# Convolving parts two at a time in a fused convolution and mixture-of-experts kernel, with 36 instead of 44 pair blocks

## The chip, the core and the metric

The kernel runs on one core of a Trainium2 chip. Five engines work at once and meet through semaphores: TensorE (PE in the profile, with its weight loads as PEld), VectorE (DVE), ScalarE (ACT), GpSimd (POOL) and SyncE (SP), which issues most transfers. The metric is the device time of one execution in microseconds; less is better.

## What is computed

The input has 8 sequences of 3584 tokens with 192 channels. A causal convolution with 7 taps comes first. Its weights are a softmax over the taps and are shared by the 24 channels of a head. Every token then goes to one of 8 experts:

```python
w = softmax(weight, axis=-1)                       # (8 heads, 7 taps)
y[b,s,h*24+c] = sum_k w[h,k] * xpad[b,s+k,h*24+c]
logits = y @ w_gate                                # 8 experts
local  = sigmoid(y @ w_local)
e[b,s] = argmax(logits) if s == 0 or local < 0.5 else e[b,s-1]
out    = softmax(logits)[e] * (relu(y @ w1[e]) @ w2[e])   # 192 -> 1024 -> 192
```

Everything is in 32-bit floats. The choice of expert runs along the sequence, so the tokens have to be routed in order.

## The kernel before

**Parts.** The 28672 tokens are cut into 16 parts of 1792 (128 partitions of 14 tokens). Parts 0 and 1 are convolved on TensorE at the start (`wide`). Parts 2 to 15 are convolved by `conv`: for each of 8 heads ScalarE makes the first tap (L411) and VectorE adds the other six in a chain of `scalar_tensor_tensor` (L421), each over 14 tokens x 24 channels = 336 elements per partition. `route` then computes the logits of a part (`logits`: four VectorE transposes, 48 TensorE products at L618, ScalarE's `ls` copies at L623, VectorE's `lq` transpose at L626, 16 small `lt` copies at L638 or L640), chooses experts, gives each token a slot, and puts 14 groups of rows into `to_put`. `put` (L824) sends one of these from the part's result tile to the DRAM tensor `slots` with an indirect transfer issued by GpSimd.

**Blocks.** As soon as enough tokens of an expert lie in `slots`, they make a block. First come 28 blocks of one unit (128 rows), then `PAIRED` = 44 blocks of two units ("pairs": `hidden`, `output`), then 22 blocks of four units (512 rows: `seven`, `output_late`), and at the end 5 pairs and single units (`hidden_late`, `output_late`). A block loads its expert's weights (`wb`, 1.5 MB) and its rows (`xg`, or `y_sb` in `ring` for the late blocks), transposes the rows, multiplies by w1, applies relu, multiplies by w2, scales, and `deliver` (L1070) scatters the result to the output. `seven` replaces the 8 products of 2x2 pieces of the first layer by 7, with sums that GpSimd (`combine_w`) and VectorE (`combine_x`, L1213, L1216, L1226) form.

**Order.** The order of the work is written out by hand. Within each block, `step(time)` puts pieces of `route` or `conv` into VectorE's queue: 4.8 after the hidden layer of a pair, 1.2 after its output matmuls and 3.6 behind its `o_sb` sums (L1057), and 2.4, 5.4, 2.0 and 1.8 in a block of four (`SIDE`). A piece says what it counts for: a tap of `conv` 0.6. The late blocks carry an overrun over to the next step; the pairs do not. `"hop"` ends a turn of `route` and lets `conv` have the rest of the step, `"pe"` does so until the next step that may use TensorE. `start_conv` lets a part begin when no row that still has to be put belongs to the part whose tile it takes. `ensure` issues the loads of rows up to `AHEAD` = 3 blocks ahead.

**Rooms.** The results of parts lie in four tiles `ys[0..3]`, taken in turn (`row_tile`); from part 8 on three of them turn, and the fourth is the ring of rows for the late blocks. The input `x_sb` has two buffers; `conv` issues the load of part g+1 at its fifth head.

Of the kernel before, what the change touches and what calls it, by code (L numbers as in the profile page):

```python
# [8 lines left out]
F32 = mybir.dt.float32  # L9
# [8 lines left out]
P = 128  # L18
B, S, D = 8, 3584, 192
H, KC = 8, 7  # L20
E, F = 8, 1024
GS = D // H
N = B * S
UT = 128
NT = 14
PT = P * NT
# [38 lines left out]
PADS = NPART  # L65
NARROW = 8
PAIRED = 44
LEFT4 = E * (QT // 2 + UT // 8)
# [42 lines left out]
def kernel(  # L111
    ctx: ExitStack,
    tc: tile.TileContext,
    x: bass.AP,
    xb: bass.AP,
    weight: bass.AP,
    wh: bass.AP,
# [7 lines left out]
    xs = ctx.enter_context(tc.tile_pool(name="xs", bufs=2))  # L125
    ys = [ctx.enter_context(tc.tile_pool(name=f"ys{k}", bufs=1)) for k in range(4)]
    yt = ctx.enter_context(tc.tile_pool(name="yt", bufs=1))
# [17 lines left out]
    def load_x(g):  # L145
        x_sb = xs.tile([P, NX, D], F32, name="x_sb")
        src = x[g // PER]
        win = bass.AP(tensor=src.tensor, offset=src.offset + g % PER * PT * D,
                      ap=[[NT * D, P], [1, NX * D]])
        nc.sync.dma_start(out=x_sb.rearrange("p t d -> p (t d)"), in_=win)  # L150
        return x_sb
# [68 lines left out]

    def z_tile():
        return yt.tile([P, 3 * NH * TB + NB * DR], F32, name="z")

    WIDE = 23

    def wide(g, xv, y_sb, both):
# [55 lines left out]
        yield from convolve(0, range(H))  # L282
        zy = z_tile()
        yT = zy[:, :3 * NH * TB].rearrange("p (u s) -> p u s", s=TB)
# [110 lines left out]

    def row_tile(g):
        at = g % 4 if g < NARROW else (g + 1) % 3
        return ys[at].tile([P, NB, DG], F32, name="y_sb")

    def conv(g, x_sb):  # L400
        y_sb = row_tile(g)[:, :NT, :]
        got[g] = y_sb

        def cols(h):
            return y_sb[:, :, Y0 + h * GS:Y0 + (h + 1) * GS]

        def chans(h, k):
            return x_sb[:, k:k + NT, h * GS:(h + 1) * GS]

        def first(h):  # L410
            nc.scalar.activation(cols(h), chans(h, 0), Act.Copy, scale=c[:, h, 0:1])  # L411

        first(0)
        yield 0
        for h in range(H):
            if h + 1 < H:
                first(h + 1)
            if h == H // 2 and 2 < g < NPART - 1:
                x_in[g + 1] = load_x(g + 1)
            for k in range(1, KC):  # L420
                nc.vector.scalar_tensor_tensor(cols(h), chans(h, k), c[:, h, k:k + 1],  # L421
                                               cols(h), Alu.mult, Alu.add)
                yield 0.6

# [174 lines left out]
    def logits(g, y_sb):  # L599

        z = z_tile()[:, :NT * D].rearrange("p (t d) -> p t d", d=D)
        for t in range(0, NT, TQ):
# [25 lines left out]
        lt = sm.tile([P, NT + 2, E + 1], F32, name="lt")  # L628
        aside = g > EARLY + 2
        for r in range(4):  # L630
            for j in range(4):
# [7 lines left out]
                else:  # L639
                    nc.vector.tensor_copy(dst, src)  # L640
                    yield 0.12
            if aside:
                yield "hop"
# [298 lines left out]
    blocks += [(1, 2, i, next(g for g in range(NPART) if i < TWO[g])) for i in range(TWO[-1])]  # L942
    FIRST = len(blocks)
    blocks += [(2, 4, i, next(g for g in range(NPART) if i < MID[g])) for i in range(MID[-1])]
    blocks += [(3, 4, i, LAST) for i in range(FOUR)]
# [136 lines left out]
    def ring(i):  # L1082

        if "rows" not in room:
            room["rows"] = ys[3].tile([P, NB, DG], F32, name="y_sb").rearrange("p b d -> p (b d)")
        at = (i - FIRST) % 4 * KQ * DG
        return room["rows"][:, at:at + KQ * DG].rearrange("p (k d) -> p k d", d=DG)

# [142 lines left out]
    def output_late(n, wb, xg, hT, rows_next=None, between=None):  # L1231

        for part, h in enumerate(hT):
# [38 lines left out]
    st = {"block": 0, "conv": 1, "cgen": None, "route": 1, "rgen": None, "routed": 1,  # L1272
          "due": False, "since": 0, "bank": None, "over": 0}

    def start_conv():
        g = st["conv"] + 1

        free = not any(p[0] <= g - 3 for p in to_put)
        if (st["cgen"] is None and g < NPART and g <= st["route"] + LEAD and free
                and (g != 3 or g in x_in and st["block"] > LATE + 2)):  # L1280
            st["conv"] = g
            st["cgen"] = conv(g, x_in.pop(g))
            next(st["cgen"])

    def conv_op():
        c = next(st["cgen"], None) if st["cgen"] else None
        if c is None:
            st["cgen"] = None
        return c

    def start_route():
        done = st["conv"] - (st["cgen"] is not None)
        if st["rgen"] is None and st["route"] < done:
            st["route"] += 1
            st["rgen"] = route(st["route"])
# [34 lines left out]

    ya, yb = row_tile(0), row_tile(1)
    hot = hotp.tile([P, 2, NB, UT], F32, name="hot")
# [33 lines left out]
    def ensure(i):  # L1366

        for j in range(len(xgs) + i, min(i + AHEAD + 1, len(blocks))):
            g = blocks[j][3]
# [45 lines left out]
    for i, (_, n, _, _) in enumerate(blocks):  # L1415
# [15 lines left out]
        if i < FIRST:  # L1431
            hT = hidden(n, wbs[i], xT, (1, 1) if i else (0, 0))
            if i < FIRST - 1:
                xT, copied = turn(n_next, xgs[i + 1])
                if len(to_put) > NT // 2 and n == KT:
                    put(copied)
# [95 lines left out]


def _block_layout(np, x):

# [43 lines left out]
```

## Time and profile before

| quantity | value |
|---|---|
| median of 4 runs | 1300.29 us (1299.66 to 1304.92) |
| the profiled execution | 1301.73 us, of which 1299.9 us is the span from the first to the last instruction |
| granted TensorE clock, mean | 0.996 |
| 0 to 211 us: parts 0 to 2, single units | PE busy 201.5 of 211.0 us |
| 211.3 to 695 us: the 44 pairs | PE busy 483.7 of 483.7 us, DVE 412.6, ACT 261.1, POOL 206.2 |
| 695 to 927 us: blocks of four beside convolution and routing | PE busy 229.8 of 232.0 us, DVE 193.9, ACT 139.8 |
| 927 to 1152.9 us: the other blocks of four | PE busy 225.9 of 225.9 us, DVE 111.4, ACT 126.0 |
| 1152.9 to 1300 us: last pairs and single units | PE busy 135.4 of 147.1 us |

The page gives each engine's busy time and the costliest groups of instructions. The view by stretches gives the same for chosen stretches of the span, and the view of waits who waited for whom. A TensorE instruction's end is modelled, so what counts is when the next one starts. A busy engine that no one waits for costs nothing.

### The profile page before, as it was taken

Reading aid. Unit: us, or ns where it says so; the run is one execution under the profiler, and the core shown is the slowest. Engines: PE = TensorE matmul, PEld = TensorE weight load, DVE = VectorE, ACT = ScalarE, POOL = GpSimd, SP = SyncE. Lnnn points to the kernel's source line nnn. Section 1 sums busy time; section 2 is a strip of 40 time slices with the busy share of each in tenths; the row PEclk is TensorE's granted clock in tenths of the full one; section 3 lists DMA queues with packets and bytes.
Section 4 is the critical chain, followed back from the end, with each engine's and each line's share of the span. In section 5 each row is a group of like instructions: output and inputs, shape, how many; then the busy total and the mean of one; then the engine's idle time right before and its main releaser. Section 6 shows DMA issues by size and latency. Waiting matters only on the chain.

```text
span 1299.9 us, 40433 instructions
## 1 busy us (share of the span) xinstructions
PE 1276.6 (98%) x16218; PEld 1233.5 (95%) x16218; DVE 908.9 (70%) x2513; ACT 703.9 (54%) x1573; POOL 547.4 (42%) x615
## 2 busy tenths in 40 slices
PE   9899999999999999999999999999999999999996
PEld 7799999999999999999999999999999999999996
DVE  6989898888888888798888888988378433310000
ACT  5456564545564646556465666575655556544453
POOL 4455352434434344444436625534536643321111
PEclk9999999999999999999999999999999999999998
DMA  5899998757766657767674435243433433325684
GB/s 198 292 348 417 389 380 323 271 195 257 271 245 221 254 209 269 268 210 266 211 282 153 167 137 172 97 143 115 150 123 129 160 105 135 111 99 187 238 305 160
DMA packets 59619, 281.52 MB, mean 217 GB/s; under 512 B 11680, under 2 KB 31191, under 8 KB 43554
## 3 DMA queue, kind: packets, MB, share of 16 engines
q1 hardware_dynamic: 37104, 233.66, 50.0%
q0 software_dynamic: 22320, 45.22, 9.4%
q8 instruction: 130, 2.13, 0.7%
q14 instruction: 63, 0.52, 0.1%
q10 hardware_dynamic: 2, 0.00, 0.0%
HBM read 233.25 MB, written 46.07 MB: 215 GB/s over the span
## 4 chain that ended last, share of the span: by engine, by line
PE 86%; issue 7%; DVE 3%; POOL 1%; DMA 1%; POOLq 0%; ACT 0%; SPq 0%; DVEq 0%
PE yps L1043 24%; PE hps L1024 23%; PE ps L1243 18%; PE ps L1194 13%; PE xps L1194 3%; PE xps L392 2%; POOL out_dram L1070 1%; PE hps L618 1%; DVE y_sb L421 1%; PE ps L1144 1%; DMA wb<-in_w_dram 1%; DMA out_dram<-o_sb,y_sb 1%; PE hps L242 1%; PE hps L187 0%; DVE hot L584 0%
## 5 line engine op out<-in xcount | busy, mean ns | idle before, releaser
L421 DVE SCALAR_TENSOR_TENSOR y_sb<-x_sb,c,y_sb 128x336 f32<-128x336 f32 x672 | 382.7, 578 | 39.0 <-ACT y_sb L411 21.3
L1043 PE MATMUL yps<-wb,hT 64*128 64x192 f32 x3712 | 323.4, 326 | 2.1 <-DVE o_sb L1057 2.0
L1024 PE MATMUL hps<-xT,wb 64*128 64x256 f32 (+1 forms) x3456 | 319.3, 336 | 1.7 <-DVE at L513 1.2
L1043 PEld LDWEIGHTS yps<-wb,hT 64*128 64x128 f32 x3712 | 305.0, 188 | 3.8 <-DVE o_sb L1057 2.3
L1024 PEld LDWEIGHTS hps<-xT,wb 64*128 64x128 f32 x3456 | 285.4, 187 | 24.2 <-issue 3.0
L1243 PE MATMUL ps<-wb,hot 64*128 64x192 f32 x3616 | 303.9, 323 | 0.0
L824 POOL DMA_INDIRECT slots<-y_sb,posi x228 | 226.3, 993 | 169.9 <-ACT xT L1010 72.3
L1243 PEld LDWEIGHTS ps<-wb,hot 64*128 64x128 f32 x3616 | 296.4, 187 | 0.7 <-issue 0.6
L1070 POOL DMA_INDIRECT out_dram<-o_sb,y_sb x113 | 117.2, 1037 | 294.6 <-DVE o_sb L1258 279.4
L1070 POOL DMA_INDIRECT out_dram<-o_sb,xg x116 | 120.8, 1041 | 240.7 <-DVE o_sb L1057 196.7
L1031 ACT ACTIVATE hT<-hps 128x512 f32<-128x512 f32 (+1 forms) x288 | 132.3, 511 | 153.2 <-PE hps L1024 153.2
L1258 DVE SCALAR_TENSOR_TENSOR o_sb<-ps,y_sb,o_sb 128x192 f32<-128x192 f32 x113 | 42.4, 411 | 206.6 <-ACT o_sb L1253 199.5
L1253 ACT ACTIVATE o_sb<-ps,y_sb 128x192 f32<-128x192 f32 x113 | 42.2, 418 | 148.9 <-PE ps L1243 144.8
L1053 ACT ACTIVATE o_sb<-yps,xg 128x192 f32<-128x192 f32 x116 | 44.0, 418 | 131.4 <-PE yps L1043 131.4
L1010 ACT COPY xT<-xps 64x256 f32<-64x256 f32 (+4 forms) x288 | 106.8, 371 | 9.6 <-PE xps L392 5.2
L1124 ACT COPY xT<-xps 64x512 f32<-64x512 f32 (+6 forms) x168 | 86.2, 513 | 2.2
L1194 PE MATMUL ps<-xT,wb 64*128 64x256 f32 x704 | 84.8, 376 | 0.0
L1194 PEld LDWEIGHTS ps<-xT,wb 64*128 64x128 f32 x704 | 73.7, 187 | 1.6 <-issue 0.3
L1144 PE MATMUL ps<-xT,wb 64*128 64x128 f32 (+1 forms) x960 | 70.1, 298 | 1.2 <-DMA wb<-in_w_dram 1.2
L1144 PEld LDWEIGHTS ps<-xT,wb 64*128 64x128 f32 x960 | 68.1, 188 | 1.8 <-ACT o_sb L1253 1.3
L1057 DVE SCALAR_TENSOR_TENSOR o_sb<-yps,xg,o_sb 128x192 f32<-128x192 f32 x116 | 44.1, 411 | 31.1 <-ACT o_sb L1053 30.7
L411 ACT ACTIVATE y_sb<-x_sb,c 128x336 f32<-128x336 f32 x112 | 63.0, 580 | 0.5
(283 smaller groups left out, 1335.7 us busy)
## 6 DMA issues: line engine op xcount, KB each, us to landing
wb<-in_w_dram SPq DMA_DIRECT2D x110, 1536.0 KB
x_sb<-in_x_dram SPq DMA_DIRECT2D x14, 1920.0 KB
xg<-slots SPq DMA_DIRECT2D x44, 195.0 KB
y_sb<-slots SPq DMA_DIRECT2D x22, 390.0 KB
wb<-in_w_dram SPq DMA_DIRECT2D x12, 512.0 KB
slots<-y_sb,posi POOLq DMA_INDIRECT x228
x_sb<-in_xb_dram SPq DMA_DIRECT2D x4, 768.0 KB
xg<-slots SPq DMA_DIRECT2D x26, 97.5 KB
```

Of the source, the lines that this page charges most:

```text
L411: nc.scalar.activation(cols(h), chans(h, 0), Act.Copy, scale=c[:, h, 0:1])
L421: nc.vector.scalar_tensor_tensor(cols(h), chans(h, k), c[:, h, k:k + 1], cols(h), Alu.mult, Alu.add)
L824: ins = nc.gpsimd.indirect_dma_start(out=slots[:, :], in_=rows, in_offset=None, out_offset=bass.IndirectOffsetOnAxis(ap=to, axis=0)).ins
L1010: copied = nc.scalar.copy(a, b)
L1024: ins = nc.tensor.matmul(hps[half][:, j, w], lhsT=wb[rows, f0:f0 + P], rhs=xT[rows, d, w], start=(d == 0 and j == 0), stop=(d == KD - 1), ...
L1031: relu = nc.scalar.activation(hT[:, m:m + 2, w], hps[half][:, :, w], Act.Relu)
L1043: ins = nc.tensor.matmul(yps[half][:, k * D:(k + 1) * D], lhsT=hT[rows, m, k * P:(k + 1) * P], rhs=wb[rows, WA + m * D:WA + (m + 1) * D], ...
L1070: sent = nc.gpsimd.indirect_dma_start(out=out, in_=o, in_offset=None, out_offset=bass.IndirectOffsetOnAxis(ap=xg.bitcast(I32)[:, k, IX:], ...
L1124: copied = nc.scalar.copy(a, b)
L1144: nc.tensor.matmul(hps[:, half, j, :], lhsT=wb[rows, f0:f0 + P], rhs=xT[rows, d, :], start=(d == 0 and j == 0), stop=(d == KD - 1), skip_g ...
L1194: ins = nc.tensor.matmul(to[:, half, j, :], lhsT=b[rows, j * P:(j + 1) * P], rhs=a[rows, :], start=(first and j == 0), stop=True, skip_gro ...
L1243: ins = nc.tensor.matmul(yps[:, half, k * D:(k + 1) * D], lhsT=h[two][rows, side, j, k * P:(k + 1) * P], rhs=wb[rows, WA + f * D:WA + (f + ...
```

## The change

- Parts 6 to 15 are convolved two at a time. One unit `(g, g+1)` goes through the 8 heads; each instruction now covers both parts, 28 x 24 = 672 elements. The planner counts 1.0 for such a tap. Parts 2 to 5 are convolved as before. Each part is still routed by itself, but only once its unit is done (`st["done"]`).
- The input of these parts comes from a new array `xd`, laid out by head on the host, so that one `x_sb` buffer holds heads 0 to 3 of both parts and the next heads 4 to 7. Loads are issued at the third and the seventh head.
- The four result tiles become one tile `rooms` for 4 x 14 rows and one tile `third` for 14 rows. A unit takes half of `rooms`; `ROOM` says where, `CLEAR` which parts have to be routed and put before. `z` gets a smaller tile, and the big `z` of the start lies in `rooms`.
- The ring of late rows lies in `third`: three places of four units instead of four; blocks of four look 2 blocks ahead instead of 3.
- The 16 `lt` copies of a part go to ScalarE only while a convolution is under way, else to VectorE, and they are cut by two hops into groups of eight, not by four into groups of four.
- A put behind a pair's row copies is made when more than 2 groups wait, before when more than 7.
- 36 pairs instead of 44, and so 26 blocks of four instead of 22.

```diff
-NARROW = 8
-PAIRED = 44
+WIDER = 6
+PAIRED = 36
@@ load_x
+        if g >= WIDER:
+            nc.sync.dma_start(out=x_sb.rearrange("p t d -> p (t d)"), in_=xd[g - WIDER])
+            return x_sb
...
+    rooms = ys.tile([P, 4 * NT, DG], F32, name="y_sb")
+    third = ys.tile([P, NT, DG], F32, name="y3")
...
-    def row_tile(g):
-        at = g % 4 if g < NARROW else (g + 1) % 3
-        return ys[at].tile([P, NB, DG], F32, name="y_sb")
-
-    def conv(g, x_sb):
-        y_sb = row_tile(g)[:, :NT, :]
-        got[g] = y_sb
+    UNITS = [(g,) for g in range(2, WIDER)] + [(g, g + 1) for g in range(WIDER, NPART, 2)]
+    ROOM = {2: None, 3: 3 * NT, 4: 0, 5: NT}
+    CLEAR = {2: -1, 3: 0, 4: 0, 5: 1}
+    for u, parts in enumerate(UNITS):
+        if len(parts) > 1:
+            ROOM[parts[0]] = (1 - u % 2) * 2 * NT
+            CLEAR[parts[0]] = parts[0] - 3
+    next_x = list(range(4, NPART))
+
+    def conv(parts):
+        g, n = parts[0], len(parts)
+        y2 = (third if ROOM[g] is None else rooms[:, ROOM[g]:ROOM[g] + n * NT, :]).rearrange(
+            "p (a t) d -> p a t d", a=n)
+        for a in range(n):
+            got[g + a] = y2[:, a]
...
         def chans(h, k):
-            return x_sb[:, k:k + NT, h * GS:(h + 1) * GS]
+            if n == 1:
+                return x_in[g][:, k:k + NT, h * GS:(h + 1) * GS]
+            x_sb = x_in[g + h // HH].rearrange("p t d -> p (t d)").rearrange(
+                "p (h a t c) -> p h a t c", h=HH, a=n, c=GS)
+            return x_sb[:, h % HH, :, k:k + NT, :]
...
-            if h == H // 2 and 2 < g < NPART - 1:
-                x_in[g + 1] = load_x(g + 1)
+            if h in ((H // 2,) if n == 1 else (HH // 2, HH + HH // 2)) and g > 2 and next_x:
+                x = next_x.pop(0)
+                x_in[x] = load_x(x)
...
-                yield 0.6
+                yield 0.6 if n == 1 else 1.0
@@ logits
-        aside = g > EARLY + 2
+        aside = g > EARLY + 2 and st["cgen"] is not None
...
-            if aside:
+            if aside and r % 2:
                 yield "hop"
@@ ring
-        at = (i - FIRST) % 4 * KQ * DG
+        at = (i - FIRST) % 3 * KQ if past < 0 else ((LATER - FIRST) % 3 * KQ + past * KT) % (3 * KQ)
@@ start_conv
-        free = not any(p[0] <= g - 3 for p in to_put)
+        free = st["routed"] >= CLEAR[g] and not any(p[0] <= CLEAR[g] for p in to_put)
@@ ensure
-        for j in range(len(xgs) + i, min(i + AHEAD + 1, len(blocks))):
+        for j in range(len(xgs) + i, min(i + (AHEAD if blocks[i][1] < KQ else 2) + 1, len(blocks))):
...
-                if len(to_put) > NT // 2 and n == KT:
+                if len(to_put) > 2 and n == KT:
                     put(copied)
```

## The prediction

> **What bounds the kernel now.** I read the page first, then stretches of single blocks, then TensorE's waits, then timelines.
>
> ```profile
> span 1299.9 us, 40433 instructions
> ...
> PE 1276.6 (98%) x16218; PEld 1233.5 (95%) x16218; DVE 908.9 (70%) x2513; ACT 703.9 (54%) x1573; POOL 547.4 (42%) x615
> ```
>
> TensorE starts work without a break; the other engines have room on the whole. The stretches are one pair, one undisturbed block of four, and four blocks of four beside routing:
>
> ```profile
> core 0: us, PE busy (x) PEld busy (x) DVE busy (x) ACT busy (x) POOL busy (x), PEclk, DMA share, GB/s
> 232.69:243.36 10.67, 10.67 (x124) 10.15 (x123) 9.65 (x19) 5.91 (x13) 5.28 (x5) 1.00 0.80 287
> 1030.57:1050.99 20.42, 20.42 (x236) 20.39 (x234) 8.01 (x12) 11.23 (x15) 11.99 (x13) 1.00 0.47 162
> ...
> 715.35:737.49 22.14, 22.14 (x331) 20.86 (x330) 20.00 (x33) 12.97 (x20) 14.05 (x15) 1.00 0.41 137
> 737.49:758.71 21.22, 20.67 (x236) 20.03 (x235) 16.22 (x28) 16.66 (x35) 6.25 (x8) 1.00 0.57 210
> 758.71:779.79 21.08, 20.66 (x236) 20.33 (x235) 17.71 (x58) 11.45 (x16) 8.61 (x10) 1.00 0.34 114
> ...
> 820.62:844.63 24.01, 22.82 (x332) 21.55 (x330) 23.35 (x39) 13.13 (x20) 14.50 (x15) 1.00 0.37 122
> ```
>
> A pair costs 10.67 us and a block of four 20.42 us for the same rows as two pairs. A logits step adds 1.73 us (22.15, seen undisturbed as 22.14). Beyond that, the block at 737 us lost 0.80, the one at 759 us 0.66, the one at 821 us 1.86. What TensorE waited for between 211 and 1152 us:
>
> ```profile
> engine line waited for: us in total, times, longest us
> PE ps L1194 <- DVE hot L1216: 1.0, 2, 0.5
> PE xps L392 <- DVE hot L1213: 0.7, 1, 0.7
> PE ps L1194 <- issue: 0.6, 1, 0.6
> ```
>
> All lie in the blocks of four; for 211 to 695 us, the pairs, the same view is empty. So pairs run at TensorE's pace, though VectorE is nearly full there:
>
> ```profile
> 222.68 0.74 DVE L1057 SCALAR_TENSOR_TENSOR o_sb<-yps,xg,o_sb 128x192 f32<-128x192 f32 x2 [1.93 <-ACT o_sb L1053]
> 223.34 9.47 DVE L421 SCALAR_TENSOR_TENSOR y_sb<-x_sb,c,y_sb 128x336 f32<-128x336 f32 x16
> 233.34 0.74 DVE L1057 SCALAR_TENSOR_TENSOR o_sb<-yps,xg,o_sb 128x192 f32<-128x192 f32 x2 [0.54 <-ACT o_sb L1053]
> ```
>
> Sixteen taps take 9.47 us (0.585 each, chained), and 0.54 us is left in the pair. VectorE may also run late: after a pair full of routing its `o_sb` came at 279.81, while TensorE's output matmuls had been issued from 271.87 to 277.29, and TensorE only needs those banks at 282.53:
>
> ```profile
> 271.87 5.42 PE L1043 MATMUL yps<-wb,hT 64*128 64x192 f32 x64
> ...
> 282.53 5.42 PE L1043 MATMUL yps<-wb,hT 64*128 64x192 f32 x64
> ```
>
> On time is 0.48 us behind the outputs' end; TensorE stalls when `o_sb` starts later than about 4.5 us.
>
> **The change, part by part.**
>
> *36 pairs, 26 blocks of four.* Eight pairs (85.36 us) become four blocks of four (81.68 us): 3.7 us less on TensorE. Everything else it issues stays, and nothing hides this, since TensorE is the path. GpSimd gets four more rounds of `combine_w` (16 sums of 0.75 us) into blocks where it is busy 8 to 12 of 20.42 us.
>
> *The two-part tap.* No row shows 672 elements. The second of two adjacent `o_sb` sums (192 elements) begins 0.33 us after the first (0.74 for two, 0.41 for one), a free tap (336 elements) 0.485 us after the one before it: 1.05 ns per element and 0.13 us fixed. The chain adds 0.12 us to five of six taps (0.605 between starts), hence the mean of 0.585. 336 more elements give 0.585 + 0.353 = 0.94 us. Lower end 0.71 (elements alone), upper end 1.17 (two old taps); I take 0.94, as two rows of the same operation lie on that line. 240 such taps replace 480: VectorE does 55 us less in all.
>
> [...]
>
> *What that does to a pair.* A tap counts 1.0 instead of 0.6, so 4.8, 1.2 and 3.6 admit 5 + 2 + 4 = 11 taps, not 8 + 2 + 6 = 16. VectorE then needs 11 x 0.94 + 0.66 (the pair's 10.67 less 0.54 less 9.47) = 11.0 us: 0.33 us more than TensorE. The saving is not spent as slack; VectorE becomes slower than TensorE while it convolves. The order in which the changed kernel's instructions stand shows three such pairs in a row (the 36th to 38th block) behind a pair full of routing and one of 4 taps and 30 routing pieces. The routing pair leaves `o_sb` 2.5 us late, as at 279.81; the mixed one measured 9.34 us with 5 old taps, so 10.2 now: 2.0 us late; three pairs later 3.0. Under 4.5, so TensorE does not wait for `yps`. Later chains start from less.
>
> *A new wait there.* In the next block ScalarE's first taps of parts 8 and 9 sit behind the last put of part 5 (GpSimd's 1.0 us issue, and 2.1 us from issue to the last packet for the put at 361.94). They are released about 3 us into the output matmuls; with the first tap's own 1.0 us and five taps of 0.94, `o_sb` starts about 3.4 us late. The `lq` transpose waits behind it, so ScalarE's eight `lt` copies (0.22 each) and a first tap stand in front of that pair's relus, which come about 1 us too late for TensorE. I charge 1.0 us, between 0 (if ScalarE catches up in the four `hps` banks) and 3 (each of three such starts). The other starts of units have under 1.5 us of lateness: nothing.
>
> *Copies in groups of eight.* In the old block at 737 us, four `lt` copies and a first tap stood before ScalarE's copy of `ps`:
>
> ```profile
> 737.71 0.73 ACT L1253 ACTIVATE o_sb<-ps,y_sb 128x192 f32<-128x192 f32 x2 [4.96 <-PE ps L1243]
> 738.33 0.89 ACT L638 COPY lt<-lq 32x36 f32<-32x36 f32 x4
> 739.23 0.58 ACT L411 ACTIVATE y_sb<-x_sb,c 128x336 f32<-128x336 f32 x1
> 739.71 0.99 ACT L1200 COPY hot<-ps 128x1024 f32<-128x1024 f32 x1
> ```
>
> That was the 0.80. After the two other logits steps only the four copies stood there: 0.21 each (20.63 at 845 and 928 us). In the new order eight copies stand there twice: 0.21 + 0.89 = 1.1 each, 2.2 in all. The last two parts are copied on VectorE, which has room: nothing.
>
> *VectorE late in blocks of four.* The 0.66 and 1.86 came from it; the 1.86 followed a 2.25 us wait for a part's first tap. `SIDE` admits 11.6 counts: 19.3 x 0.585 = 11.3 us before, 11.6 x 0.94 = 10.9 now, and one unit starts in this stage where two parts did. I take 0; the upper end is the old 2.5.
>
> *Loads.* A unit's second `x_sb` is needed 6 taps after its load stands in the program, but SyncE issues it at the block's start: for parts 6 and 7 some 16 us ahead. In the trace the packets of these loads (the only ones of 15360 bytes) ended 11.4 to 14.5 us after issue. Hidden; if the margin of 2 us fails, ScalarE stands and the cost is what is missing. The ring of three and two blocks of looking ahead still give a row load some 20 us. The earlier puts, the rooms and `z` move no instruction in front of TensorE's. Part 15's routing ends as many blocks before its rows are needed as before.
>
> **Sum**, against the profiled execution's 1301.7 us (span 1299.9 and 1.8 around): -3.7 (fewer products), -3.7 (old stalls 0.80 + 0.66 + 1.86 + 2 x 0.21), +2.2 (groups of eight), +1.0 (late relus), 0 (VectorE) = -4.2, so 1297.5. That execution was 1.4 us over the median of 1300.3; against the median it is 1296.1.
>
> **Rivals.**
>
> *Stalls move, and only the products remain (within 0.3%).* The old stalls come back at other blocks. For: VectorE and ScalarE carry as much per block of four as before, and one block now holds 20.5 us of VectorE work by row durations. Against: two of the old stalls have places that the new order does not have. 1300.3 - 3.7 + 0 to 3 = 1296.6 to 1300.
>
> *VectorE becomes the bound (slower).* One mechanism: the two-part tap costs more than the line says, for instance through its access over two parts. Place: the convolving pairs. From 0.98 us the chain of three pairs uses up its 4.5 us; at about 1.02 the stalls eat the gain of 4.2; from 1.05 it is slower by over 0.3%. At 1.17, 176 such taps in the pairs cost 41 us more, less some 15 us that VectorE idles there: 1300.3 - 4.2 + 26 = 1322. For: the pair is already over its pace at 0.94. Against: the row of 336 elements shows no cost for runs of 24 beyond the line through 192.
>
> *More gain.* Neither new stall shows: 1300.3 - 7.4 = 1292.9.
>
> **How the numbers follow.** 0.3% of 1300 us is 3.9 us, about what a measurement of this kernel can tell from no change. My forecast of 1296.1 lies just over that bound, so its sign against the bound is open. Chances: forecast and more gain together 0.52 (faster), stalls that move 0.25 (same), slower 0.23, of which the costly tap 0.15 and an unseen wait of ScalarE or a load 0.08. The range goes from 1292.3 (the greatest gain, and the 0.6 us by which the fastest runs lie under the median) to 1304.5 (a tap of about 1.05 us, or another 8 us of waits); beyond it lie a tap over 1.05 (0.12) and a little under it. Taken alone the forecast has 1293 to 1297.
>
> **What would show it.** Pairs still 10.67 apart, blocks of four 20.42. L440 (the tap) with 672 elements at about 0.92 us, starts 0.955 apart in a chain. `o_sb` up to 3.5 us late in the 38th and 39th block. Two blocks of four near 21.5 us after a logits step. I am wrong if TensorE waits for `o_sb` in the pairs (tap too dear), if ScalarE's first taps wait for `x_sb` or `slots` for over 2 us in front of relus, or if the blocks of four lose more than 4 us.

## The result, and the profile after

The changed kernel takes 1302.2 us (median of 40 runs, 1300.0 to 1307.1) where the kernel before takes 1301.0 (63 runs): 1.0011 times as long, 95% interval 1.0007 to 1.0016. That is within the 0.3% that the prediction took for no change, but on the slower side; the forecast was 1296.1 and faster. The time lies inside the prediction's range of 1292.3 to 1304.5, near the end that it gave to a dear tap or to 8 us of waits. A later set of 12 and 17 runs gave 1.0002 (0.9992 to 1.0011). The profiled execution took 1303.5 us (span 1301.8), 1.8 more than the one before.

From the page of the changed kernel, its span and the busy time of the engines:

```profile
span 1301.8 us, 40105 instructions
...
PE 1276.5 (98%) x16186; PEld 1226.8 (94%) x16186; DVE 893.5 (69%) x2372; ACT 689.3 (53%) x1449; POOL 586.8 (45%) x631
```

TensorE is as busy as it was, although eight pairs have become four blocks of four. The view by stretches shows one pair, one undisturbed block of four, two blocks of four behind a logits step, and last a pair of a kind that the old kernel did not have (columns: start and end, length, then busy time with instructions of TensorE, its weight loads, VectorE, ScalarE, GpSimd, then granted clock, DMA share, GB/s).

```profile
222.97:233.63 10.66, 10.66 (x122) 10.04 (x122) 9.55 (x18) 5.44 (x12) 5.29 (x6) 1.00 0.92 340
1055.78:1076.19 20.41, 20.41 (x235) 19.53 (x234) 8.00 (x12) 11.23 (x15) 7.12 (x8) 1.00 0.34 118
...
680.16:701.83 21.67, 20.66 (x236) 20.02 (x234) 16.17 (x40) 15.28 (x33) 7.54 (x8) 1.00 0.53 196
...
765.05:786.84 21.79, 20.77 (x234) 20.10 (x234) 16.18 (x36) 15.39 (x33) 9.52 (x10) 1.00 0.35 115
333.09:347.88 14.79, 12.66 (x125) 11.92 (x122) 13.47 (x20) 9.30 (x29) 2.58 (x2) 0.88 0.71 268
```

The undisturbed paces are what they were. What TensorE waited for from the first pair to the last block of four:

```profile
engine line waited for: us in total, times, longest us
PE yps L1065 <- ACT hT L1053: 3.1, 4, 2.1
PE ps L1217 <- issue: 2.0, 2, 1.0
PE hps L639 <- DVE z L625: 1.0, 1, 1.0
```

Before, this view had nothing in the pairs, and VectorE's sums (`hot`) in the blocks of four. Now it names ScalarE's relus (`hT`) in the pairs and, in the block at 459 us, VectorE's transposes for the logits (`z`), and in the blocks of four two waits of 1.0 us that the profile gives no releaser for.

To see where the time went I took each block's length, subtracted the undisturbed length (10.67 or 20.42) and 1.74 for a logits step, and summed what is left. "Front" is the time to the first pair, "tail" that behind the last block of four.

| profiled execution | front | 44 or 36 pairs: lost | 22 or 26 blocks of four: lost | pairs and blocks of four together | tail |
|---|---|---|---|---|---|
| before | 211.4 | 0.3 | 3.5 | 941.5 | 147.0 |
| after | 212.3 | 8.3 | 2.9 | 945.3 | 144.2 |
| difference | +0.9 | +8.0 | -0.6 | +3.8 | -2.8 |

The new mix of blocks stands in these numbers with its 3.7 us by construction, since the losses are counted against the undisturbed lengths: 8.0 - 0.6 - 3.7 is the +3.8 (by rounding 3.7). What supports it is that the undisturbed lengths are what they were. The pairs, where nothing was lost before, lose 8.0 us: 4.1 in the block at 333 us, 1.7 and 0.6 in those at 459 and 473, 0.5 each at 382 and 573, 0.6 in those at 527 and 561. The tail is 2.8 us shorter. The front lay between 210.8 and 213.2 in the runs of later kernels, none of which was edited there, so its 0.9 is within what single executions differ by.

**The block at 333 us**, in the timeline (start, duration, engine, line, operation; in brackets the idle time before it and what ended it):

```profile
324.19 0.98 POOL L1092 DMA_INDIRECT out_dram<-o_sb,xg  x1 [2.63 <-DVE o_sb L1079]
...
326.22 5.42 PE L1065 MATMUL yps<-wb,hT 64*128 64x192 f32 x64
...
328.47 0.96 POOL L845 DMA_INDIRECT slots<-y_sb,posi  x1 [0.30 <-issue]
...
331.00 1.62 ACT L429 ACTIVATE y_sb<-x_sb,c 128x672 f32<-128x672 f32 x2 [2.09 <-DMA slots<-y_sb,posi]
...
331.90 4.74 DVE L440 SCALAR_TENSOR_TENSOR y_sb<-x_sb,c,y_sb 128x672 f32<-128x672 f32 x5 [2.67 <-ACT y_sb L429]
336.56 0.74 DVE L1079 SCALAR_TENSOR_TENSOR o_sb<-yps,xg,o_sb 128x192 f32<-128x192 f32 x2
337.21 0.43 DVE L647 STREAM_TRANSPOSE lq<-ls 128x256 f32<-128x256 f32 x1
...
337.68 1.81 ACT L659 COPY lt<-lq 32x36 f32<-32x36 f32 x8 [3.98 <-DVE lq L647]
339.50 0.88 ACT L429 ACTIVATE y_sb<-x_sb,c 128x672 f32<-128x672 f32 x1
340.28 2.03 ACT L1053 ACTIVATE hT<-hps 128x512 f32<-128x512 f32 x4
...
340.90 7.15 PE L1065 MATMUL yps<-wb,hT 64*128 64x192 f32 x64 [2.13 <-ACT hT L1053]
```

GpSimd first issues the two scatters of the block before, for which it stood 2.63 us until VectorE's late `o_sb` was done (324.19), and then the last puts of part 5, the very last at 328.47, 2.25 us into the output matmuls (326.22). The first taps of parts 8 and 9 go into its room and stand on ScalarE until it has landed, at 331.0. VectorE has nothing to do for 2.67 us and then runs five taps in front of `o_sb`, which begins 4.9 us behind the outputs' end (331.64). `lq` follows it, eight `lt` copies and a first tap follow `lq` in ScalarE's queue, and the four relus behind them come only from 340.28 on. TensorE waits 2.13 us, but the block loses 4.1. The stretches of that block show the rest:

```profile
338.77:341.00 2.23, 0.10 (x3) 0.10 (x2) 2.16 (x3) 2.18 (x7) 1.36 (x1) 1.00 1.02 433
341.00:343.00 2.00, 2.00 (x20) 2.00 (x22) 1.93 (x3) 1.98 (x5) 0.00 (x0) 0.78 0.89 364
343.00:345.00 2.00, 2.00 (x16) 2.00 (x14) 1.93 (x4) 1.89 (x8) 0.00 (x0) 0.50 0.28 103
345.00:347.88 2.88, 2.88 (x34) 2.88 (x34) 1.88 (x5) 1.59 (x5) 0.00 (x0) 0.91 0.00 0
```

Behind the wait the granted clock falls to half and TensorE makes 16 products in 2 us. That costs another 2.0 us: PE is busy for 12.66 us in this block and for 10.66 in an undisturbed one.

**Copies in front of relus.** At 382, 473 and 573 us sixteen `lt` copies stand in a row in front of a pair's relus, at 680 and 765 us eight in front of a block of four's copies:

```profile
382.44 3.61 ACT L659 COPY lt<-lq 32x36 f32<-32x36 f32 x16
386.08 0.87 ACT L429 ACTIVATE y_sb<-x_sb,c 128x672 f32<-128x672 f32 x1
386.85 2.03 ACT L1053 ACTIVATE hT<-hps 128x512 f32<-128x512 f32 x4
...
681.00 1.80 ACT L659 COPY lt<-lq 32x36 f32<-32x36 f32 x8
682.82 1.01 ACT L1223 COPY hot<-ps 128x1024 f32<-128x1024 f32 x1
...
683.93 1.13 PE L1217 MATMUL ps<-xg 64*128 64x256 f32 x8 [1.01 <-issue]
```

**The tail.** What SyncE's queue waited for behind the last block of four, in the kernel before:

```profile
SPq L971 <- DMA out_dram<-o_sb,y_sb: 109.8, 14, 17.1
```

and in the changed one:

```profile
SPq L993 <- DMA out_dram<-o_sb,y: 19.3, 10, 3.1
```

L971 and L993 are the same load of rows into the ring. In the old ring of four places each late block took a whole place, and its load waited for the scatters that used the place before. The weight loads stand behind it in the same queue, and TensorE waited for two of them (1.2 us). The new ring gives the late blocks six places of two units; in the changed kernel TensorE waits for nothing there. Those waits and what they delay are 1.8 of the 2.8 us; the other 1.0 lies behind the last products (10.3 us before, 9.3 after) and is not the ring's, since the one later kernel with the old ring (e7) has 9.1 us there. The whole tail took 147.9 us in e7 and 143.6 to 144.2 in all that have the new one on such a chip.

### The profile page after: what moved, and what is told of

The parts are those of the page before. It is cut to its first block, busy times and chain, and to the rows that moved or that the text cites. A ratio compares the mean times of both kernels' runs of the same rounds, so it can differ in the third digit from the quotient of the medians.

```text
span 1301.8 us, 40105 instructions
## 1 busy us (share of the span) xinstructions
PE 1276.5 (98%) x16186; PEld 1226.8 (94%) x16186; DVE 893.5 (69%) x2372; ACT 689.3 (53%) x1449; POOL 586.8 (45%) x631
## 3 DMA queue, kind: packets, MB, share of 16 engines
q8 instruction: 130, 2.13, 0.7%
## 4 chain that ended last, share of the span: by engine, by line
PE 93%; DVE 3%; ACT 1%; issue 1%; DMA 0%; POOL 0%; POOLq 0%; DVEq 0%
PE ps L1266 26%; PE yps L1065 20%; PE hps L1046 18%; PE ps L1217 16%; PE ps L1167 5%; PE xps L1217 3%; PE xps L397 2%; PE hps L639 1%; ACT lt L659 1%; DVE y L440 1%; PE hps L247 1%; PE ps L639 0%; PE hps L192 0%; DVE hot L605 0%; DMA slots<-y_sb,posi 0%
## 5 line engine op out<-in xcount | busy, mean ns | idle before, releaser
L1266 PE MATMUL ps<-wb,hot 64*128 64x192 f32 x4128 | 346.0, 323 | 0.0
L1266 PEld LDWEIGHTS ps<-wb,hot 64*128 64x128 f32 x4128 | 337.6, 187 | 1.3 <-issue 0.8
L440 DVE SCALAR_TENSOR_TENSOR y_sb<-x_sb,c,y_sb 128x672 f32<-128x672 f32 (+1 forms) x384 | 302.4, 797 | 18.1 <-ACT y_sb L429 8.7
L1065 PE MATMUL yps<-wb,hT 64*128 64x192 f32 x3200 | 282.4, 328 | 6.2 <-ACT hT L1053 3.1
L1046 PE MATMUL hps<-xT,wb 64*128 64x256 f32 (+1 forms) x3072 | 277.4, 331 | 1.4 <-DVE at L534 1.2
L1065 PEld LDWEIGHTS yps<-wb,hT 64*128 64x128 f32 x3200 | 265.2, 189 | 9.0 <-ACT hT L1053 3.7
L1092 POOL DMA_INDIRECT out_dram<-o_sb,y x129 | 135.4, 1050 | 297.4 <-DVE o_sb L1281 277.0
L1281 DVE SCALAR_TENSOR_TENSOR o_sb<-ps,y,o_sb 128x192 f32<-128x192 f32 x129 | 48.4, 412 | 235.2 <-ACT o_sb L1276 235.1
L1276 ACT ACTIVATE o_sb<-ps,y 128x192 f32<-128x192 f32 x129 | 48.0, 417 | 179.1 <-PE ps L1266 174.6
L1217 PE MATMUL ps<-xg 64*128 64x256 f32 x416 | 54.6, 378 | 2.0 <-issue 2.0
```

Of the source, the lines that this page charges most:

```text
L1046: ins = nc.tensor.matmul(hps[half][:, j, w], lhsT=wb[rows, f0:f0 + P], rhs=xT[rows, d, w], start=(d == 0 and j == 0), stop=(d == KD - 1), ...
L1065: ins = nc.tensor.matmul(yps[half][:, k * D:(k + 1) * D], lhsT=hT[rows, m, k * P:(k + 1) * P], rhs=wb[rows, WA + m * D:WA + (m + 1) * D], ...
L1092: sent = nc.gpsimd.indirect_dma_start(out=out, in_=o, in_offset=None, out_offset=bass.IndirectOffsetOnAxis(ap=xg.bitcast(I32)[:, k, IX:], ...
L1217: ins = nc.tensor.matmul(to[:, half, j, :], lhsT=b[rows, j * P:(j + 1) * P], rhs=a[rows, :], start=(first and j == 0), stop=True, skip_gro ...
L1266: ins = nc.tensor.matmul(yps[:, half, k * D:(k + 1) * D], lhsT=h[two][rows, side, j, k * P:(k + 1) * P], rhs=wb[rows, WA + f * D:WA + (f + ...
L1281: nc.vector.scalar_tensor_tensor(o_sb[:, k, :], yps[:, 1, k * D:(k + 1) * D], xg[:, at + k, 0:1], o_sb[:, k, :], Alu.mult, Alu.add)
```

## The experiments

Three theories for the loss in the pairs. R (release): first taps of a unit stand on ScalarE until the puts out of their room have landed. G (groups): the `lt` copies stand in front of relus and of copies of `ps`. V (VectorE): eleven taps a pair are more than TensorE's pace allows, `o_sb` falls behind from pair to pair.

**The changed kernel again, and the mix of blocks alone.**

> The changed kernel itself, unaltered, so that the other runs have it beside them on their chip: 1.001 times the time before, as measured first.

1301.6 us, 1.0002 (0.9992 to 1.0011); pairs lose 8.1, blocks of four 2.75, in the same blocks as before.

> The kernel before with one number changed: 36 pairs and 26 blocks of four instead of 44 and 22. The prediction's first term alone: eight pairs (85.4 us) become four blocks of four (81.7 us), 3.7 us faster than before if the stalls of the blocks of four (3.7 us behind the routing and convolution of parts 12 to 15) do not grow. Rival: the blocks of four that then stand beside convolution and routing (four more of them) stall as those did, 0.2 to 1.9 us in every second one, and 2 to 4 us of it is lost: no faster than before.

The edit is to the kernel before:

```diff
-PAIRED = 44
+PAIRED = 36
```

1322.8 us, 1.0160 (1.0143 to 1.0176): 22 us slower than before. The pairs lose 0.6, one block of four loses 22.7. That block in the view by stretches, and what TensorE waited for there:

```profile
1028.57:1071.64 43.07, 23.39 (x236) 22.30 (x235) 30.12 (x143) 11.44 (x16) 25.44 (x27) 0.76 0.37 132
```

```profile
PE xps L392 <- DVE hot L1213: 19.6, 1, 19.6
```

Part 15 is not routed when its rows are due. `ensure` then puts all of its routing into VectorE's queue in front of the sum into h11 (L1213), which starts at 1054.84. Neither theory of the expectation named this. The 3.7 us of the new mix are not to be had with the old convolution: it ends too late for it.

**Fewer taps a pair.**

> The changed kernel, but the planner counts a two-part tap as 1.21 instead of 1.0, so that a convolving pair holds 4 + 1 + 3 = 8 of them (VectorE then needs 8 x 0.94 + 0.66 = 8.2 us of 10.67, and covers as many elements a pair as the kernel before did with 16 taps). Theory V: the lateness of o_sb that the three 11-tap pairs build up (2.4, 2.5, then 4.9 us in the changed kernel) is what makes lq and the relus late; with 8 taps the stalls at 333 us (4.1) and 459 us (1.7) go and it is 4 to 6 us faster. Theory R: the first taps still wait for the scatters and the wait hits ScalarE's queue as before; o_sb is on time before it, so the stall at 333 us falls from 4.1 to about 2, and each unit's convolution takes two pairs longer, which nothing waits for: 2 us faster at most.

```diff
-                yield 0.6 if n == 1 else 1.0
+                yield 0.6 if n == 1 else 1.21
```

1339.3 us, 1.0293 (1.0278 to 1.0309). The pairs lose 2.7 instead of 8.3, but three blocks of four lose 14.0, 11.2 and 17.8:

```profile
PE xps L397 <- DVE hot L1236: 35.0, 3, 15.5
```

It is the mechanism of the run above, three times over. That "each unit's convolution takes two pairs longer, which nothing waits for" was wrong: with 36 pairs there is no room for a slower convolution. As the units now start at other blocks, the run does not tell R from V.

> The changed kernel with the overrun of a pair's steps carried over to the next step while a unit is convolved and a two-part tap counted as 0.92: on the average 10.4 taps a pair instead of 11, VectorE 10.4 x 0.94 + 0.66 = 10.5 us of 10.67. With 36 pairs the last rows would then be routed too late by the planner's own order, so it has 38 pairs and 25 blocks of four, which the first term prices at 0.9 us slower. Theory V: o_sb no longer falls behind from pair to pair, the stalls near 333 and 458 us shrink by 3 us or more together: 2 us faster than the changed kernel or better. Theory R and G: the starts of units and the groups of eight are unchanged: 1 us slower.

```diff
-PAIRED = 36
+PAIRED = 38
...
-                yield 0.6 if n == 1 else 1.0
+                yield 0.6 if n == 1 else 0.92
...
-        st["over"] = min(time, 0) if late_p else 0
+        st["over"] = min(time, 0) if late_p or st["unit"] > 4 and st["cgen"] is not None else 0
```

1305.4 us, 1.0035 (1.0020 to 1.0051): 3 to 4 us slower than the changed kernel, where V said 2 faster, R and G 1 slower. The lateness that builds up from pair to pair is not needed for such a stall: `o_sb` is on time up to the start of the unit (331.62, 0.49 us behind the outputs' end, where the changed kernel had 2.5), and the block behind that start still loses 5.2 us:

```profile
331.62 0.74 DVE L1079 SCALAR_TENSOR_TENSOR o_sb<-yps,xg,o_sb 128x192 f32<-128x192 f32 x2 [2.44 <-ACT o_sb L1075]
...
340.17 0.87 ACT L429 ACTIVATE y_sb<-x_sb,c 128x672 f32<-128x672 f32 x1 [1.10 <-DMA slots<-y_sb,posi]
341.06 0.43 ACT L644 COPY ls<-hps 128x128 f32<-128x128 f32 x2
...
347.15 1.82 ACT L659 COPY lt<-lq 32x36 f32<-32x36 f32 x8 [2.80 <-DVE lq L647]
348.98 0.87 ACT L429 ACTIVATE y_sb<-x_sb,c 128x672 f32<-128x672 f32 x1
349.86 1.80 ACT L659 COPY lt<-lq 32x36 f32<-32x36 f32 x8
351.68 2.06 ACT L1053 ACTIVATE hT<-hps 128x512 f32<-128x512 f32 x4
```

The last put has landed 2.1 us into the outputs (340.17 against 338.11), earlier than in the changed kernel, but the first tap also stands in front of the logits' `ls` copies, and now sixteen `lt` copies in front of the relus. So this stall has R and G in it, and is not the one at 333 us over again.

**A later start of units.** The same edit ran twice, as e1 and e8; e1 to e4 are told at the end of this section.

> The kernel of e1 (a unit of two parts starts no earlier than the third planning step behind the last put of the part in its room) on a chip where the kernel before takes about 1301 us. Theory R: no first tap stands before landed scatters any more, the stalls near 333 us (4.1) and 458 us (1.5 to 1.7) go, and unless the first taps then fall between other ScalarE work it is 5 us faster than the changed kernel, near 1296.5. Theory V: o_sb is already 2.4 us late in front of the unit start, and the later start leaves the pairs behind it as full as they were: 2 us faster at most. The stalls move: a new one of 3 to 4 us appears where two first taps and eight lt copies stand together in front of a block of four's copies, and nothing is gained.

```diff
 def put(behind=None):
         g, rows, to = to_put.pop(0)
+        last[g] = st["steps"]
...
 def start_conv():
+        free = free and (len(parts) == 1 or st["steps"] > last.get(CLEAR[g], -9) + 2)
...
 def step(...):
+        st["steps"] += 1
```

1298.6 us, 0.9979 (0.9970 to 0.9988): 3 us faster than the changed kernel and faster than the one before. The pairs lose 0.9 instead of 8.3; nothing is left at 333 and 459 us, although `o_sb` is as late in front of them (2.5 us) as it was. What TensorE waited for from the first pair to the last block of four, and ScalarE in the block at 333 us:

```profile
PE ps L1218 <- issue: 4.2, 2, 2.5
PE yps L1066 <- ACT hT L1054: 0.3, 1, 0.3
```

```profile
335.09 1.80 ACT L659 COPY lt<-lq 32x36 f32<-32x36 f32 x8
336.90 0.87 ACT L429 ACTIVATE y_sb<-x_sb,c 128x672 f32<-128x672 f32 x1
337.67 1.07 ACT L1054 ACTIVATE hT<-hps 128x512 f32<-128x512 f32 x2
```

The eight `lt` copies and a first tap still stand in front of the relus, but the relus begin 4.1 us into the block (it starts at 333.61), where they began 7.2 us into it. So R holds for the pairs: with the lateness of V and with the copies there is no stall at the starts of units once no first tap waits. But the blocks of four lose 6.7 instead of 2.9: one of them 4.4, where a first tap, eight `lt` copies and another first tap now stand in front of its copies. Part of the gain moved on, as the third case of the expectation said.

> The changed kernel with the later start of units (behind the o_sb sums) in the pairs alone; the unit that starts in a block of four starts as in the changed kernel. Theory R: the pairs lose about 1 us instead of 8.0 as in e8, and the blocks of four 3.2 us instead of e8's 7.0: 6 to 7 us faster than the changed kernel, 1295 to 1296. If e8's dear block of four came from something else than the place of that start, it stays: 1298.6 as e8.

(Against the edit of e8.)

```diff
-        free = free and (len(parts) == 1 or st["steps"] > last.get(CLEAR[g], -9) + 2)
+        free = free and (len(parts) == 1 or late_p or st["steps"] > last.get(CLEAR[g], -9) + 2)
```

1300.3 us, 0.9995 (0.9986 to 1.0004), 4 to 5 us above what R said. The pairs lose 0.8, as expected, but the blocks of four 7.8, of which one 6.3. The last unit now starts later than in the changed kernel whatever the rule in this stage, since the one before it ended later: its first taps stand behind ScalarE's row copies, VectorE's eight taps follow, `o_sb`, `lq` and `lt` come late, and TensorE stands 3.5 us until the block's first copy of `ps` is done.

**Copies elsewhere.**

> The changed kernel, but ScalarE's lt copies may be issued only in those planning steps that stand behind a pair's relus and row copies (the 4.8 step), or in a block of four not in the last step in front of its copies; sixteen together in a pair, eight together in a block of four. Theory G: the stalls near 382 (0.49), 472 (0.64), 573 (0.50), 679 (1.25) and 764 us (1.38) go, and of the 4.1 near 333 us the share of its eight copies in front of the relus (1.8): 4 to 6 us faster than the changed kernel, 1296 to 1298. If the time of ScalarE was not the cause, but o_sb and lq late on VectorE: 2 us faster at most, and the relus still come late near 333 us.

```diff
 def step(time, bank=None, early=0, force=False, act=True):
+        st["act"] = act
...
         for r in range(4):
+            while aside and r % 2 == 0 and not st["act"] and st["cgen"] is not None:
+                yield "hop"
...
-            if aside and r % 2:
+            if aside and r % 2 and late_p:
                 yield "hop"
```

`act` is False in the 1.2 and the 3.6 step of a pair and in the last step of a block of four. 1312.2 us, 1.0084 (1.0070 to 1.0098): about 10 us slower than the changed kernel. The pairs lose 18.7. The relus are no longer late, but TensorE waits for `o_sb`:

```profile
PE yps L1067 <- DVE o_sb L1081: 8.5, 5, 2.1
```

```profile
382.90 0.27 DVE L674 TENSOR_REDUCE mx<-lt 128x14 f32<-128x112 f32 x1 [4.05 <-ACT lt L661]
```

With the hop behind the copies gone, the first reduction of `lt` stood in VectorE's queue right behind them and waited 4.05 us for all sixteen, with `o_sb` behind it. The edit made this wait itself, so it says nothing against G; it shows what the hop is there for. In the blocks of four, where the hop had stayed, 2.3 are lost.

> The edits of e8 and e10 together. R and G both right: the pair stalls (8.0 us in all) and those behind logits steps in the blocks of four (2.6) go but for about 1: 8 to 9 us faster than the changed kernel, near 1293, and faster than the kernel before. If stalls only move: within 3 us of the changed kernel.

(The edits of e8 and e10.) 1308.9 us, 1.0062 (1.0048 to 1.0076): the pairs lose 16.8 by the same wait for `lt`, the blocks of four 0.9.

> The changed kernel, but in blocks of four no lt copy of ScalarE is issued in the last planning step of a block, in front of the next block's three copies of ps; the copies then stand eight behind those copies and eight behind the row copies. The pairs are untouched. Theory G for the blocks of four: the stalls at 679 us (1.25) and 764 us (1.38) go, 2.6 us faster than the changed kernel, near 1299 on a chip where the kernel before takes 1301; the pairs lose 8.0 us as before. If the two stalls come from VectorE or from the puts, nothing changes.

(The edit of e10 with the hop as in the changed kernel, and `act` False in the last step of a block of four alone.) 1299.7 us, 0.9997 (0.9988 to 1.0006), about 1 to 2 us faster than the changed kernel. The blocks of four lose 1.3 instead of 2.9, and the two stalls of 1.25 and 1.38 are gone (a new one of 0.65 stands in the block behind the first). The pairs lose 7.7. G holds, at something over half its price.

**Both, and the price of the mix.**

> e12 and e13 together. If the two causes are apart and complete: 8.0 - 1.0 + 2.6 = 9.6 us faster than the changed kernel, 1291 to 1293, which is the prediction's sum without its two new stalls (1292.9). If they only move: 1296 or more.

(The edits of e12 and e13.) 1295.3 us, 0.9957 (0.9943 to 0.9970): 6 to 7 us faster than the changed kernel and 5.5 faster than the one before, the best version of the study. The pairs lose 0.85 and the blocks of four 2.7, nearly all of it (2.6) at the start of the last unit. So the two causes together carry 11.2 - 3.6 = 7.6 of the 11.2 us that the changed kernel loses in pairs and blocks of four; they were not quite apart, since the later start in the pairs pushes the last unit into a worse place.

> e14 with 44 pairs and 22 blocks of four. The prediction's first term alone: 3.7 us slower than e14. If the routing that then falls into more pairs costs waits, more than 3.7; if the blocks of four beside routing lose as much as the pairs gain, less.

```diff
-PAIRED = 36
+PAIRED = 44
```

1297.8 us, 0.9978 (0.9968 to 0.9987), 2.5 us slower than e14. Its pairs and blocks of four take 941.0 us together where those of e14 take 937.6: 3.4 more, with 3.3 us lost where e14 loses 3.55. That these make 3.7 us together says only that the undisturbed lengths are the same in both, since the losses are counted against them. The measured 2.5 us go the way of the first term; from five and ten runs their size is not known better than to about 2 us.

**Four runs on a slower chip.** e1 to e4 ran on a chip where the kernel before took 1326.2 us (29 runs). TensorE stands for "issue" there, for which the profile shows no cause, in many places: 16.7 us in all in e1, of which 7.1 lie ahead of 212 or behind 1160 us, and 11.4 in e2, where the changed kernel has 3.2 on a faster chip. The changed kernel itself was not run there.

> The changed kernel, but a unit of two parts may start only from the third planning step behind the last put of the part that lay in its room; in a pair that is the step behind the o_sb sums, half a pair later. Theory R (release): the stalls of the blocks at 333 us (4.1), 459 us (1.7), 527 us (0.3) and 561 us (0.2) of the changed kernel's trace come from ScalarE's first taps, which stand in its queue until the last scatter out of the room has landed. They should go: about 6 us faster than the changed kernel, near 1296. Theory G (groups of eight): the main cause at 333 us are the eight lt copies in front of the relus, which are still there: 2 us faster at most. Theory V (VectorE overfull with 11 taps a pair): o_sb is late before the unit starts, and a later start only moves the lateness: no change, or up to 2 us slower because the convolution ends later.

(The edit of e8.) 1325.3 us, 0.9988 (0.9975 to 1.0001).

```profile
PE ps L1218 <- issue: 5.5, 5, 2.5
PE yps L1066 <- issue: 3.3, 7, 0.8
```

> The changed kernel with one line as before: a hop behind every four lt copies instead of every eight. Theory G: the stalls that stand in blocks right behind a logits step, at 382 us (0.49), 473 us (0.64), 573 us (0.50), 680 us (1.25, of which four copies alone would cost 0.21) and 765 us (1.38, likewise) go but for 2 x 0.21: 3.8 us faster than the changed kernel, near 1298.4; the one at 333 us (4.1) loses up to 0.9, four copies, in front of its relus. Theory R and theory V: the same 3.8 at most, and the 4.1 at 333 us stays whole.

```diff
-            if aside and r % 2:
+            if aside:
                 yield "hop"
```

1324.1 us, 0.9978 (0.9961 to 0.9994).

> Both edits at once. If R and G are right and independent: 6.3 + 3.8 = 10 us faster than the changed kernel, near 1292. If the stalls only move to other blocks: 3 us faster or less. Theory V: stalls of o_sb in the pairs stay.

1327.6 us, 1.0012 (0.9999 to 1.0025): the two edits together do worse than each alone.

> The changed kernel with 44 pairs and 22 blocks of four, as before the change. The prediction's first term says 3.7 us slower than the changed kernel (four blocks of four at 20.42 us become eight pairs at 10.67), near 1305.9, if the stalls stay as they are: those at 333 and 459 us stand in pairs either way; those at 680 and 765 us (1.25 + 1.38) stand behind logits steps that would now fall into pairs, where such a step cost about 0.5, so 1.6 of it could come back: 2 to 4 us slower.

1334.2 us, 1.0056 (1.0034 to 1.0078).

These are inconclusive. Without the changed kernel beside them their differences from it are not known, and what a block loses there mixes the edits with the chip. Hops by four were not tried on the other chip; whether they alone would do stays open. e15 puts the question of e4 to the kernel of e14.

## Why the prediction was wrong

Most terms came out. The sum failed in what ScalarE's queue costs the pairs: it charged 1.0 us, and 8.0 were lost. Of the 7.0 between, the start of a unit at 333 us has 3.1, the other starts 2.0, and copies that stood in no term 1.6.

- *36 pairs, 26 blocks of four, -3.7.* It holds as far as the runs show: a pair still took 10.66 us and a block of four 20.41, and e15, with the old mix, was 2.5 us slower than e14. That GpSimd's additional sums cost nothing held too. What the forecast did not say is that this term hangs on the pace of the convolution (e7: +22 us with the old one, e6: +38 with fewer taps a pair).
- *Old stalls, -3.7.* Right for 3.3 of it: the waits for VectorE's sums are gone from the blocks of four. Two losses of 0.2 us remain, now in the two blocks that hold a logits step (658 and 743 us).
- *The two-part tap, 0.94 us.* Right: 0.919 us median, 0.954 between starts in a chain, where 0.92 and 0.955 were forecast. Eleven taps a pair, and `o_sb` 2.4 and 2.5 us late in the pairs at 305 and 316 us, without a wait, about as written (2.0 rising to 3.0).
- *Copies in groups of eight, +2.2.* The mechanism and its two places were right; they cost 1.25 + 1.38 = 2.6 where 1.1 each stood. But the same copies, sixteen in a row in front of the relus of the pairs at 382, 473 and 573 us, were not in the sum at all: 0.49 + 0.64 + 0.50 = 1.6.
- *"I charge 1.0 us, between 0 ... and 3".* This is the step that failed. The chain was the right one, link by link: put, first taps, taps, `o_sb`, `lq`, `lt`, relus. Its first link was too short: the release was put "about 3 us into the output matmuls" and came 4.8 us into them (331.00 against 326.22), because GpSimd first issued the two scatters of the block before, which waited for a late `o_sb`. The prediction had that lateness of `o_sb` on VectorE, but did not carry it into GpSimd's queue. So `o_sb` was 4.9 us late and not 3.4, the relus 2.1 us and not 1, and the half clock behind that wait, which the prediction had not priced, doubled the price: 4.1 us, more than the upper bound gave to three starts together. One of the prediction's signs of being wrong had come: first taps that wait for `slots` for over 2 us (2.09) in front of relus.
- *"The other starts of units have under 1.5 us of lateness: nothing."* Wrong for the same reason. The start at 459 us left `o_sb` 5.1 us late and cost 1.7, the one at 561 us 3.3 us late and 0.3. The other 0.3, at 527 us, stands in a block in which no unit starts; its cause stays open.
- *VectorE late in blocks of four, 0.* Right.
- *Loads and the ring, "hidden".* Right for the stages with convolution, wrong for the tail, where the new places freed SyncE's queue: 1.8 of the 2.8 us, which were in no term.

Against the forecast's -4.2 the two traces differ by +1.9. Of the 6.1 between, the pairs give 8.0 - 1.0 = 7.0, the blocks of four 0.9 (-0.6 against -1.5), the front 0.9, the tail -2.8. The likeliest rival, that stalls move, is nearest to what happened, but these were not the old stalls at other blocks: they came from ScalarE's queue, in the pairs, and were more than that rival's 0 to 3 us. VectorE did not become the bound, its tap was as cheap as forecast.

## What to carry to other kernels

An instruction that waits for a transfer should not be queued on an engine in front of work that TensorE needs: the wait is paid by all that stands behind it, here through five links, and moving the start of the unit half a block later removed nearly all of it in the pairs (0.9 us lost instead of 8.3), though part came back in the blocks of four (6.7 instead of 2.9). If a wait of TensorE is to be priced, price the clock behind it too: here waits of about 2 us cost 2.6 us in one place and 4.1 and 4.2 in two others. And where a faster stage pays only by letting another setting move (the 36 pairs), run that setting alone: it shows whether the gain is a sum of two or a product of both.

## What the runs showed of the hardware

Two stretches of the changed kernel, each right behind a wait of TensorE of 1.0 us:

```profile
465.50:472.71 7.21, 7.15 (x153) 6.68 (x154) 7.00 (x9) 2.38 (x6) 5.48 (x5) 1.00 0.76 305
...
684.00:690.00 6.00, 6.00 (x68) 5.96 (x70) 3.57 (x4) 5.46 (x13) 2.62 (x4) 1.00 0.57 200
```

- Waits of about 1.0 us left the granted clock at 1.00. Behind the wait of 2.13 us it went to 0.78, 0.50 and 0.91 in stretches of 2.0, 2.0 and 2.9 us, which is 3.4 us at half speed: (0.22 x 2.0 + 0.50 x 2.0 + 0.09 x 2.88) x 2. In the kernel of e9 a wait of 3.3 us cost 5.2, in that of e13 waits of 0.67 and 3.47 us cost 6.3.
- The length of a wait does not decide alone. In the kernel of e10 a wait of 2.07 us ends at 389.94 and one of 2.08 us at 599.34, both for `o_sb`; behind the first the clock is halved, behind the second it is not:

```profile
389.86:393.27 3.41, 3.33 (x20) 3.33 (x22) 3.06 (x15) 0.16 (x1) 2.80 (x3) 0.50 0.18 60
...
598.07:601.48 3.41, 2.14 (x26) 2.14 (x28) 3.20 (x14) 1.30 (x3) 1.94 (x2) 1.00 0.10 34
601.48:604.89 3.41, 3.41 (x45) 3.41 (x43) 3.02 (x17) 0.36 (x2) 2.50 (x4) 1.00 0.24 83
```

- The two blocks lose 4.2 and 2.6 us. In the kernel before the clock falls to half once ahead of the last products, at 64.08 us, and in the changed kernel twice, at 65.62 and 342.10, each time for 3.41 us. The wait ahead of it was for `o_sb` at the first two (2.0 and 2.2 us) and for `hT` at the third (2.13 us). From the kernel before:

```profile
53.84:57.25 3.41, 1.68 (x24) 1.70 (x25) 2.99 (x18) 1.71 (x7) 2.23 (x3) 1.00 0.59 136
57.25:60.67 3.42, 3.42 (x59) 3.42 (x58) 3.15 (x10) 1.53 (x4) 0.67 (x1) 1.00 1.01 384
60.67:64.08 3.41, 1.43 (x21) 1.13 (x20) 3.30 (x7) 2.19 (x7) 0.17 (x1) 1.00 1.06 425
64.08:67.50 3.42, 3.42 (x26) 3.42 (x24) 3.24 (x7) 0.00 (x0) 2.78 (x3) 0.50 1.02 420
```

and from the changed one:

```profile
62.21:65.62 3.41, 1.21 (x15) 1.18 (x16) 3.27 (x8) 1.76 (x6) 0.96 (x1) 1.00 1.07 422
65.62:69.03 3.41, 3.41 (x27) 3.41 (x25) 3.27 (x6) 0.79 (x2) 2.00 (x3) 0.50 0.99 400
338.69:342.10 3.41, 1.28 (x18) 1.20 (x16) 3.30 (x4) 3.36 (x9) 1.44 (x1) 1.00 0.97 413
342.10:345.51 3.41, 3.41 (x26) 3.41 (x24) 3.30 (x5) 3.25 (x12) 0.00 (x0) 0.50 0.41 158
```

- In the step of 3.41 us right ahead of these three, TensorE stood for 1.98, 2.20 and 2.13 us; in the step of the kernel before at 53.84 us it stood for 1.73, and the clock stayed at 1.00. The two falls of the changed kernel lie 276.48 us apart, 81 times 3.413. Counted on in such steps from 389.86, in the kernel of e10, 598.07 is a boundary, and it cuts the second wait into 0.8 and 1.3 us, while the first lies almost wholly inside one step. An estimate from these few stretches: what counts is how long TensorE stands within one step, and it was chance that the 2.13 us at 333 us cost 4.1, since they lie inside one (338.77 to 340.90). No run was made to try it.
- A put took GpSimd 0.96 us in some places and, after the change, 1.4 to 1.6 us in others; before, none took longer than 1.31 us. The mean rose from 0.99 to 1.09 us. The 46 longer ones all stand beside two-part taps on VectorE (300.17, 305.51, 316.29 us among them). Whether the taps cause it was not tried. The late release at 331 us is not theirs: GpSimd stood idle for 2.63 us between them and the scatters.
